# Attention scores of two heads in one product: keys in two zero-padded slots, heads rearranged between row halves

## The chip, the cores and the metric

The kernel runs on one core of a Trainium2 chip. The core has a matrix engine (TensorE, PE in the profile; PEld are its weight loads), VectorE (DVE), ScalarE (ACT), GpSimd (POOL) and a queue engine (SyncE, SP) that issues most transfers. A matrix product reads a stationary operand (`lhsT`) and a moving operand (`rhs`) from on-chip memory, contracts over the partitions, which are the rows of the array, and writes to PSUM; the columns of the stationary operand become the partitions of the output. The metric is the time of one execution on the device in microseconds (us); lower is better.

## What is computed

A sparse attention of 8 batches with 8 heads each (576 positions, 64 elements per head), and behind it a mixture of 8 experts over its 4,608 rows. Heads 0 to 3 use a local mask (a position sees itself and the 31 before it), heads 4 to 7 a strided mask (it sees earlier positions of the same residue modulo 32).

```python
scores = scale * np.matmul(q, k.transpose(0, 1, 3, 2))
mask_local = (rel >= 0) & (rel < stride)
mask_strided = (rel >= 0) & (pos[None, :] % stride == pos[:, None] % stride)
...
attn = np.exp(scores - max) / sum
x = (attn @ v) as rows of 512
out[do_compute] = xc + gate * (relu(xc @ w1[e]) @ w2[e])
```

## The kernel before

Positions of the strided heads are stored by residue, so that both masks become bands: a local block is 64 queries against a window of 96 keys (9 blocks), a strided block is 54 queries against 54 keys (11 blocks of three residues). The heads of one kind come in four to a batch and lie in a tile as two row halves `i` (partitions 0 to 63 and 64 to 127) times two columns `j`. A batch is cut into four units, `UNITS`: local blocks 0 to 4, local 5 to 8, strided 0 to 5, strided 6 to 10; unit (b, pr) is piece pr of batch b. All 32 units go through the same stages:

- `qk` makes the scores S: for each block four products, one per head, with 64 rows of contraction, 64 output columns and 96 or 54 moving columns (line 186). The four use the four quarters of the array, since head (i, j) reads row half i and writes output half i^j. The output has two PSUM banks (bank j) and one buffer. VectorE adds the mask (lines 193 and 195) and reduces the maximum (201), GpSimd subtracts it (204).
- `tex` transposes the differences on TensorE (224), ScalarE takes exp (232) into `ptl` or `pts`. For the strided kind two blocks stand in the 64-wide slots of `frame` and are transposed together; the odd block of the last unit has two transposes of its own.
- `pv` multiplies with the values and a column of ones (258). VectorE divides by the sum (266, 267, 273) into `x`.
- `xpose` transposes `x` (300), `score` computes gate logits from it (325), `route1` and `route2` make the slot of every row, and `scat` writes slot tables by indirect transfers of GpSimd (419).

The loop over units (from line 787) issues `qk` two units ahead (`LA = 2`): at unit n stand, on TensorE, S of unit n+2, then transposes of n, PV of n-1, transposes of the outputs of n-2. The order on TensorE, VectorE and GpSimd is as the code is written (`manual_schedule`); an engine waits at its next instruction until what it needs is there.

Loads stand in SP's queue in program order. A tile of queries and one of keys for each batch and kind come from one pool of six buffers (`part`, line 144), so three pairs are held; `loadq` (157) and `loadk` (162) issue two transfers each, one per `j` over 128 partitions. At odd units the loop loads the pair that is used three units later. `loadv` (167) loads values one batch ahead. Each transfer waits also for the transfer eight earlier (`DMAHW`), so at most eight are in flight. After the attention the feed-forward part runs (lines 603 to 605); the weights of the first expert are loaded during the last batches of the attention.

```python
p = slice(HP * i, HP * i + HP)
T.matmul(s[HP * (i ^ j):HP * (i ^ j) + HP, j, (blk - b0) * win:(blk - b0 + 1) * win],
         lhsT=qt[p, j, blk * nq:blk * nq + HP], rhs=kt[p, j, blk * nq:blk * nq + win],
         start=True, stop=True)
```

Of the kernel before, what the change touches and what calls it, by code (L numbers as in the profile page):

```python
# [23 lines left out]
HP = 64  # L24
# [73 lines left out]
def attn_moe(ctx: ExitStack, tc: tile.TileContext, q, k, v, w9d, w1d, w2d, cst, out, NB=B):  # L98
# [41 lines left out]
    frame = [ap.tile([128, 2, 6, HP], F32, name=f"frame{i}") for i in range(2)]  # L140

    qt_, kt_, vt_ = {}, {}, {}

    def part(d, L, kind, name):
        t = zp.tile([128, 2, S + PAD], F32, name=f"{name}{kind}", tag="qk", bufs=6)[:, :, 0:L[kind]]
        return t, d[:, :, kind * L[0]:kind * L[0] + L[kind]].rearrange("j p c -> p j c")

    def qtile(b, kind):
        qt_[b, kind], d = part(q[b], QL, kind, "qt")
        return qt_[b, kind], d  # L150

    def ktile(b, kind):
        kt_[b, kind], d = part(k[b], KL, kind, "kt")
        return kt_[b, kind], d

# [6 lines left out]
    def loadk(b, kind):  # L162
        t, d = ktile(b, kind)
        for j in range(2):
            nc.sync.dma_start(t[:, j], d[:, j])
# [10 lines left out]
    def qk(b, pr):  # L176
        kind, b0, b1 = UNITS[pr]
        qt, kt = qt_[b, kind], kt_[b, kind]
        nq, win = ((HP, LW), (SQ, SQ))[kind]
        n = (b1 - b0) * win  # L180
        s = ps("S", 2)
        for blk in range(b0, b1):
            for j in range(2):
                for i in range(2):
                    p = slice(HP * i, HP * i + HP)
                    T.matmul(s[HP * (i ^ j):HP * (i ^ j) + HP, j, (blk - b0) * win:(blk - b0 + 1) * win],  # L186
                             lhsT=qt[p, j, blk * nq:blk * nq + HP], rhs=kt[p, j, blk * nq:blk * nq + win],
                             start=True, stop=True)
# [13 lines left out]
        e = sw if kind == 0 else frame[pr - 2][:, :, 0:b1 - b0, 0:win]  # L202
# [6 lines left out]
    def tex(b, pr):  # L209
        kind, b0, b1 = UNITS[pr]  # L210
        e = e_.pop((b, pr))
        if kind == 0:
            pt = ap.tile([LW, 5 * 2 * 128], F32, name="ptl", tag="ptl", bufs=2)
            jobs = [(e[:, j, blk, :], LW) for blk in range(b1 - b0) for j in range(2)]
        else:
            pt = ap.tile([128, 3 * 2 * 128], F32, name="pts", tag="pts", bufs=2)
            fr = frame[pr - 2]
            jobs = [(fr[:, j, 2 * p:2 * p + 2, :].rearrange("p n w -> p (n w)")[:, 0:w], w)
                    for p in range((b1 - b0 + 1) // 2) for w in [HP + SQ if 2 * p + 1 < b1 - b0 else SQ] for j in range(2)]
        for g in range(0, len(jobs), 4):  # L220
            t = ps("T")
            part = jobs[g:g + 4]
            for x, (a, w) in enumerate(part):
                T.transpose(t[:w, x * 128:(x + 1) * 128], a, ident)  # L224
            yield
            x = 0
            while x < len(part):
                w = part[x][1]
                y = x
                while y < len(part) and part[y][1] == w:  # L230
                    y += 1
                A.activation(pt[:w, (g + x) * 128:(g + y) * 128], t[:w, x * 128:y * 128], AF.Exp, scale=0.125)
                x = y
        pt_[b, pr] = pt.rearrange("p (n j i q) -> p n j i q", j=2, i=2, q=HP)
# [3 lines left out]
    def pv(b, pr):  # L238
# [7 lines left out]
        if kind == 0:  # L246
            jobs = [(0, LW, m, j, j, m) for m in range(n) for j in range(2)]
            slots = (n, n)
            outs = [x[:, :, 64 * j:64 * j + 64] for j in range(2)]
        else:  # L250

            jobs = [(HP * o, HP * o + SQ, m, j, o, 2 * m + j) for m in range((n + 1) // 2)
                    for o in range(2) for j in range(2) if 2 * m + o < n]
            slots = (n + 1) // 2 * 2, n // 2 * 2
            outs = [x[:, o::2, :].rearrange("p m (j d) -> p m j d", j=2) for o in range(2)]
# [808 lines left out]
```

## Time and profile before

| | |
|---|---|
| median of 3 runs | 451.42 us (451.34 to 454.69) |
| the profiled execution | 449.82 us, of which the span of the profile is 448.2 us |
| mean granted TensorE clock | 0.975 |
| attention | up to about 181.5 us of the span |
| feed-forward | 181.5 to 448 us |

The profile lists every instruction with its start and duration; a group such as `x48` is 48 records, and a product of 32-bit floats leaves two records on TensorE (640 score products, 1,280 records). The chain of waits is followed back from the last instruction: each step names what released the next one; "issue" in it is time in which the engine waited for nothing that the profile shows. The DMA share is the mean busy share of 16 transfer engines.

### The profile page before, as it was taken

How to read it: one execution, taken by the hardware profiler on the slowest of the kernel's cores; microseconds unless marked ns; L12 is line 12 of the kernel's file. 1: busy time of each engine (PE TensorE's matmuls, PEld its weight loads, DVE VectorE, ACT ScalarE, POOL GpSimd, SP SyncE). 2: the span in 40 equal slices, each digit the busy share in tenths (PEclk: the TensorE clock that was granted, in tenths of full speed). 3: DMA queues.
4: the chain of work that ended last, by engine and by line, in shares of the span. 5: the costliest groups of instructions: out<-in, count | busy, mean ns of one | idle time of the engine just before them, and what ended most of it. 6: DMA issues, size and time to landing. Idle time of an engine off the chain costs nothing.

```text
span 448.2 us, 12126 instructions
## 1 busy us (share of the span) xinstructions
PE 413.8 (92%) x4951; PEld 370.7 (83%) x4952; DVE 257.6 (57%) x521; ACT 187.3 (42%) x366; POOL 163.9 (37%) x205
## 2 busy tenths in 40 slices
PE   6989889988878888899999999999999999999995
PEld 3867768766666666789899799999999999999984
DVE  3675667666857864481477465464474564756611
ACT  1345344533443625551543343444444444544400
POOL 3443236663658584464024318014024022200201
PEclk9799999998999879999999999999999999999999
DMA  8999999989798324532547466446566466645201
GB/s 298 398 393 335 361 322 351 289 261 317 211 348 261 102 57 108 147 67 79 181 158 220 149 217 207 153 159 207 171 197 184 159 200 198 214 157 158 73 21 42
DMA packets 53465, 91.09 MB, mean 203 GB/s; under 512 B 9272, under 2 KB 29624, under 8 KB 53406
## 3 DMA queue, kind: packets, MB, share of 16 engines
q1 hardware_dynamic: 45725, 79.86, 54.4%
q0 software_dynamic: 7680, 10.42, 8.3%
q8 instruction: 40, 0.66, 0.6%
q14 instruction: 20, 0.16, 0.1%
HBM read 75.22 MB, written 15.63 MB: 203 GB/s over the span
## 4 chain that ended last, share of the span: by engine, by line
PE 80%; DMA 7%; issue 5%; ACT 2%; DVE 2%; SPq 1%; POOL 1%; POOLq 0%; DVEq 0%; ACTq 0%
PE S L603 16%; PE S L605 16%; PE S L604 16%; PE PV L258 8%; PE S L186 5%; PE T L224 5%; DMA vt<-in_vp_dram 5%; PE T L300 4%; PE T L325 3%; PE PV L695 2%; PE T L597 2%; DMA kt<-in_kp_dram 2%; DMA xg<-out_dram,tab 1%; ACT s L330 1%; ACT xT L302 1%
## 5 line engine op out<-in xcount | busy, mean ns | idle before, releaser
L683 POOL DMA_INDIRECT out_dram<-ot,tab x25 | 28.0, 1120 | 150.7 <-DVE ot L681 142.1
L603 PE MATMUL S<-xh,w1h 128*128 128x342 f32 (+6 forms) x248 | 78.6, 317 | 0.2 <-DVE hl L616 0.2
L605 PE MATMUL S<-xh,w1l 128*128 128x342 f32 (+6 forms) x248 | 76.6, 309 | 0.0
L604 PE MATMUL S<-xl,w1h 128*128 128x342 f32 (+6 forms) x248 | 76.5, 308 | 0.0
L603 PE MATMUL S<-hh,w2h 128*128 128x288 f32 (+5 forms) x192 | 59.4, 309 | 0.0
L604 PE MATMUL S<-hl,w2h 128*128 128x288 f32 (+5 forms) x192 | 57.9, 302 | 0.0
L605 PE MATMUL S<-hh,w2l 128*128 128x288 f32 (+5 forms) x192 | 57.9, 302 | 0.0
L615 ACT ACTIVATE hh<-S 128x342 fp32r<-128x342 f32 (+6 forms) x64 | 28.0, 437 | 64.0 <-PE S L605 57.0
L541 DVE TENSOR_TENSOR w1l<-raw,w1h 128x1024 fp32r<-128x1024 f32 x32 | 40.4, 1266 | 22.0 <-ACT w1h L535 19.2
L603 PEld LDWEIGHTS S<-xh,w1h 128*128 128x128 f32 x248 | 46.8, 189 | 1.2 <-issue 0.6
L604 PEld LDWEIGHTS S<-xl,w1h 128*128 128x128 f32 x248 | 46.9, 189 | 0.1
L605 PEld LDWEIGHTS S<-xh,w1l 128*128 128x128 f32 x248 | 46.8, 189 | 0.0
L541 DVE TENSOR_TENSOR w2l<-raw,w2h 128x1024 fp32r<-128x1024 f32 x32 | 39.0, 1223 | 10.3 <-ACT w2h L535 10.1
L419 POOL DMA_INDIRECT table<-pay,rdi x38 | 40.3, 1060 | 12.1 <-issue 8.8
L575 POOL DMA_INDIRECT xg<-out_dram,tab x25 | 32.6, 1304 | 33.2 <-DMA out_dram<-ot,tab 9.9
L186 PE MATMUL S<-kt,qt 64*64 64x54 f32 (+1 forms) x1280 | 34.6, 245 | 9.2 <-issue 4.4
L616 DVE SCALAR_TENSOR_TENSOR hl<-S,hh 128x342 fp32r<-128x342 f32 (+6 forms) x64 | 31.0, 484 | 20.8 <-ACT hh L615 18.0
L186 PEld LDWEIGHTS S<-kt,qt 64*64 64x64 f32 x1280 | 28.1, 142 | 16.3 <-issue 6.8
L204 POOL TENSOR_TENSOR sm<-sm,mx 128x480 f32<-128x480 f32 (+1 forms) x32 | 28.4, 911 | 27.1 <-DVE mx L201 20.6
L603 PEld LDWEIGHTS S<-hh,w2h 128*128 128x128 f32 x192 | 36.2, 188 | 0.1
L604 PEld LDWEIGHTS S<-hl,w2h 128*128 128x128 f32 x192 | 36.3, 189 | 0.0
L605 PEld LDWEIGHTS S<-hh,w2l 128*128 128x128 f32 x192 | 36.2, 189 | 0.0
(159 smaller groups left out, 782.6 us busy)
## 6 DMA issues: line engine op xcount, KB each, us to landing
raw<-in_w_dram SPq DMA_DIRECT2D x64, 512.0 KB
vt<-in_vp_dram SPq DMA_DIRECT2D x40, 390.0 KB
qt<-in_qp_dram SPq DMA_DIRECT2D x16, 304.0 KB
kt<-in_kp_dram SPq DMA_DIRECT2D x16, 297.0 KB
out_dram<-x SPq DMA_DIRECT2D x16, 288.0 KB
kt<-in_kp_dram SPq DMA_DIRECT2D x14, 304.0 KB
qt<-in_qp_dram SPq DMA_DIRECT2D x14, 288.0 KB
out_dram<-x SPq DMA_DIRECT2D x32, 99.0 KB
```

Of the source, the lines that this page charges most:

```text
L186: T.matmul(s[HP * (i ^ j):HP * (i ^ j) + HP, j, (blk - b0) * win:(blk - b0 + 1) * win], lhsT=qt[p, j, blk * nq:blk * nq + HP], rhs=kt[p, j ...
L204: G.tensor_tensor(e[:, j], sw[:, j], mx[:, j].unsqueeze(2).broadcast_to([128, b1 - b0, win]), op=ALU.subtract)
L258: T.matmul(p[HP * i:HP * i + HP, bank, slot * 65:slot * 65 + 65], lhsT=pt[a:z, m, j, i ^ j, :], rhs=vt[a:z, (b0 if kind == 0 else b0 // 2) ...
L419: i = G.indirect_dma_start(out=table, out_offset=bass.IndirectOffsetOnAxis(ap=di[:, t:t + 1], axis=0), in_=pay[:, t, :], in_offset=None, b ...
L541: V.tensor_tensor(lo, raw_.pop((key, j)), hi.bitcast(F32), op=ALU.subtract)
L575: i = G.indirect_dma_start(out=xg[:s["P"], t, :], out_offset=None, in_=out[0:last, :], in_offset=bass.IndirectOffsetOnAxis(ap=s["tab"][:s[ ...
L603: T.matmul(p, lhsT=a[0], rhs=b[0], start=start, stop=False)
L604: T.matmul(p, lhsT=a[0], rhs=b[1], start=False, stop=False)
L605: T.matmul(p, lhsT=a[1], rhs=b[0], start=False, stop=stop)
L615: A.activation(s["hh"][:, f, :C], p[:, :C], AF.Relu)
L616: V.scalar_tensor_tensor(s["hl"][:, f, :C], p[:, :C], 0.0, s["hh"][:, f, :C].bitcast(F32), op0=ALU.max, op1=ALU.subtract)
L683: i = G.indirect_dma_start(out=out, in_=ot[:P], in_offset=None, bounds_check=NTOK - 1, oob_is_err=False, out_offset=bass.IndirectOffsetOnA ...
```

## The change

Keys get one tile per kind, `kz`, instead of a buffer of the pool: 128 partitions, two columns `j`, two slots `i`. Row half i holds its keys in slot i, and zeros stand in the other slot (four memsets, two by GpSimd, two by VectorE, once at the start). One product now contracts over all 128 rows with the queries of both halves and has the two slots as its moving operand, so that it gives the scores of two heads side by side: 192 or 108 moving columns instead of 96 or 54, two products for a block instead of four, each with 64 output columns (output half j). The heads in `q` and `k` are laid out so by the host (`pack`). Scores are stored in `segments`, (block, head) one after the other over the two banks; a block whose two segments fall into different banks (one local block of unit 0, one strided block of unit 3) keeps four products with half the rows.

`loadk` writes 64 partitions per transfer, both `j`. As each kind has one key tile, its next load waits until the products of the last unit that reads it are done, and is written behind that unit's `qk` in the program (`loadk(1, 0)` behind the two first `qk`, the loop's at the end of the odd unit). `loadq` keeps three buffers of its own. `tex` of the strided kind transposes slots 2m and 2m+1, two heads of one block: five transposes in the last unit of a batch instead of six. `pv` takes the matching order, and in the last unit of a batch VectorE has one pair of small operations for the sums (lines 266 and 267) where it had two.

```diff
-    frame = [ap.tile([128, 2, 6, HP], F32, name=f"frame{i}") for i in range(2)]
+    frame = [ap.tile([128, 12, HP], F32, name=f"frame{i}") for i in range(2)]
...
+    kz = [zp.tile([128, 2, 2, n], F32, name=f"kz{kind}") for kind, n in enumerate(KL)]
...
+        qt_[b, kind] = t = zp.tile([128, 2, S + PAD], F32, name=f"qt{kind}", tag="qt", bufs=3)[:, :, 0:QL[kind]]
...
-    def loadk(b, kind):
-        t, d = ktile(b, kind)
-        for j in range(2):
-            nc.sync.dma_start(t[:, j], d[:, j])
+    def loadk(b, kind, c=slice(0, None)):
+        d = k[b][:, :, kind * KL[0]:kind * KL[0] + KL[kind]].rearrange("j p c -> p j c")
+        for i in range(2):
+            p = slice(HP * i, HP * i + HP)
+            nc.sync.dma_start(kz[kind][p, :, i, c], d[p, :, c])
+
+    def segments(pr):
+        _, b0, b1 = UNITS[pr]
+        seq = [(blk, i) for blk in range(b0, b1) for i in range(2)]
+        if pr == 0:
+            seq.insert(b1 - b0, seq.pop(1))
+        return {x: divmod(f, b1 - b0) for f, x in enumerate(seq)}
...
         for blk in range(b0, b1):
+            (x, at), (x1, _) = seg[blk, 0], seg[blk, 1]
             for j in range(2):
+                if x == x1:
+                    T.matmul(s[HP * j:HP * j + HP, x, at * win:(at + 2) * win], lhsT=qt[:, j, blk * nq:blk * nq + HP],
+                             rhs=kt[:, j, :, blk * nq:blk * nq + win], start=True, stop=True)
+                    continue
                 for i in range(2):
...
+                    p, c = slice(HP * i, HP * i + HP), i ^ j
+                    x, at = seg[blk, i]
+                    T.matmul(s[HP * c:HP * c + HP, x, at * win:(at + 1) * win], lhsT=qt[p, c, blk * nq:blk * nq + HP],
+                             rhs=kt[p, c, i, blk * nq:blk * nq + win], start=True, stop=True)
+                x, x1 = 0, 1
...
-            jobs = [(fr[:, j, 2 * p:2 * p + 2, :].rearrange("p n w -> p (n w)")[:, 0:w], w)
...
+            jobs = [fr[:, 2 * HP * m:2 * HP * m + HP + SQ] for m in range(b1 - b0)]
...
+    for kind in range(2):
+        G.memset(kz[kind][0:HP, :, 1], 0.0)
+        V.memset(kz[kind][HP:128, :, 0], 0.0)
...
-    loadk(1, 0)
     loadv(0, 1)
...
     run(qk(0, 1))
+    loadk(1, 0)
...
                 loadq(g // 2, g % 2)
-                loadk(g // 2, g % 2)
...
         run(*rank, *late, *front)
+        if pr % 2 and n // 2 + 3 < 2 * NB:
+            loadk((n // 2 + 3) // 2, (n // 2 + 3) % 2)
```

How the program order changes on two engines. First TensorE around the strided units of batch 1 and the first unit of batch 2, before (S are scores, T transposes or small sums, PV the products with values; a row is a run of equal instructions, and `64x54` is output partitions times moving columns):

```order
L186 MATMUL S<-kt_250,qt_247 64x54 x24
L224 MATMUL T<-cs,sm_80 96x128 x10
L258 MATMUL PV<-vt_134,pts 64x65 x20
L300 MATMUL T<-cs,x_437 128x128 x6
L186 MATMUL S<-kt_250,qt_247 64x54 x20
L224 MATMUL T<-cs,sm_81 96x128 x8
L258 MATMUL PV<-vt_196,ptl 64x65 x20
L300 MATMUL T<-cs,x_437 128x128 x5
L186 MATMUL S<-kt_406,qt_403 64x96 x20
```

The same place after the change:

```order
L188 MATMUL S<-kz_87,qt_224 64x108 x12
L235 MATMUL T<-cs,sm_80 96x128 x10
L256 MATMUL PV<-vt_137,pts 64x65 x20
L292 MATMUL T<-cs,x_385 128x128 x6
L188 MATMUL S<-kz_87,qt_224 64x108 x4
L194 MATMUL S<-kz_87,qt_224 64x54 x4
L188 MATMUL S<-kz_87,qt_224 64x108 x4
L235 MATMUL T<-cs,sm_81 96x128 x8
L256 MATMUL PV<-vt_185,ptl 64x65 x20
L292 MATMUL T<-cs,x_385 128x128 x5
L194 MATMUL S<-kz_86,qt_363 64x96 x4
L188 MATMUL S<-kz_86,qt_363 64x192 x8
```

The stages stand in the same order. Inside a score stage there are half as many products of twice the moving columns, and in units 0 and 3 of a batch a run of four products of the old form stands ahead of the others or between them.

Second SP's queue in the first microseconds, before (`kt_131` are the keys of batch 1, local, `vt_134` the values of batch 0, strided, `vt_196` those of batch 1, local, `kt_250` the keys of batch 1, strided):

```order
L165 DMA kt_131<-in_kp_dram 128x608 [waits DMAHW0_49]
L165 DMA kt_131<-in_kp_dram 128x608 [waits DMAHW1_49]
L172 DMA vt_134<-in_vp_dram 128x780 [waits DMAHW2_49]
L172 DMA vt_134<-in_vp_dram 128x780 [waits DMAHW3_49]
L172 DMA vt_196<-in_vp_dram 128x780 [waits DMAHW4_49]
L172 DMA vt_196<-in_vp_dram 128x780 [waits DMAHW5_49]
L172 DMA vt_196<-in_vp_dram 128x780 [waits DMAHW6_49]
L160 DMA qt_247<-in_qp_dram 128x608 [waits DMAHW7_49,PE_49]
L160 DMA qt_247<-in_qp_dram 128x608 [waits DMAHW0_49]
L165 DMA kt_250<-in_kp_dram 128x594 [waits DMAHW1_49]
L165 DMA kt_250<-in_kp_dram 128x594 [waits DMAHW2_49]
```

And after the change (`kz_86` is the local key tile, `kz_87` the strided one, `vt_137` the values of batch 0, strided, `vt_185` those of batch 1, local):

```order
L173 DMA vt_137<-in_vp_dram 128x780 [waits DMAHW2_49]
L173 DMA vt_137<-in_vp_dram 128x780 [waits DMAHW3_49]
L159 DMA kz_86<-in_kp_dram 64x2x608 [waits DMAHW4_49,PE_49]
L159 DMA kz_86<-in_kp_dram 64x2x608 [waits DMAHW5_49]
L173 DMA vt_185<-in_vp_dram 128x780 [waits DMAHW6_49]
L173 DMA vt_185<-in_vp_dram 128x780 [waits DMAHW7_49]
L173 DMA vt_185<-in_vp_dram 128x780 [waits DMAHW0_49]
L153 DMA qt_224<-in_qp_dram 128x608 [waits DMAHW1_49]
L153 DMA qt_224<-in_qp_dram 128x608 [waits DMAHW2_49]
L159 DMA kz_87<-in_kp_dram 64x2x594 [waits DMAHW3_49,PE_49]
L159 DMA kz_87<-in_kp_dram 64x2x594 [waits DMAHW4_49]
```

The keys of batch 1, local, have moved behind two transfers of values, and the loads of keys wait for TensorE where the loads of queries did.

96 lines of the change are left out of this document (36 added, 60 removed).

## The prediction, made before the changed kernel ran

> **What bounds the kernel now.** I read the page first (span, busy shares, slices, chain), then a table of stretches, one for each batch of the attention, then TensorE's waits between 27 and 160 us, then the chain in order of time.
>
> ```profile
> span 448.2 us, 12126 instructions
> PE 413.8 (92%) x4951; PEld 370.7 (83%) x4952; DVE 257.6 (57%) x521; ACT 187.3 (42%) x366; POOL 163.9 (37%) x205
> PE   6989889988878888899999999999999999999995
> DMA  8999999989798324532547466446566466645201
> PE 80%; DMA 7%; issue 5%; ACT 2%; DVE 2%; SPq 1%; POOL 1%; POOLq 0%; DVEq 0%; ACTq 0%
> ```
>
> TensorE is busy 92% of the span and makes 80% of the chain that ended last. In the slices (11.2 us each) it is at eight or nine tenths from the second on, but in the first nine slices the transfer engines are as full. So two things could set the pace of the attention.
>
> ```profile
> core 0: us, PE busy (x) PEld busy (x) DVE busy (x) ACT busy (x) POOL busy (x), PEclk, DMA share, GB/s
> 0.00:27.40 27.40, 21.48 (x405) 16.05 (x407) 15.88 (x30) 7.03 (x14) 12.29 (x31) 0.88 0.96 355
> 27.40:45.40 18.00, 17.15 (x386) 13.71 (x386) 10.51 (x25) 8.46 (x19) 6.21 (x8) 1.00 1.01 356
> 45.40:64.90 19.50, 17.65 (x399) 13.90 (x399) 11.79 (x26) 9.00 (x21) 6.21 (x8) 1.00 1.00 344
> 128.70:153.90 25.20, 20.21 (x411) 16.07 (x409) 19.61 (x52) 11.44 (x26) 16.76 (x26) 0.93 0.70 222
> ```
>
> Each stretch runs from one batch's first strided scores to the next's. From 27.4 us a batch takes 18.0 to 19.5 us, TensorE is busy 17.15 and 17.65 us of it, VectorE 10.5 to 11.8. The transfer share is 1.0 in both, so I looked at who waits for a transfer.
>
> ```profile
> PE PV L258 <- issue: 5.7, 10, 1.4
> PE S L186 <- issue: 3.8, 6, 1.8
> PE T L224 <- issue: 2.3, 6, 1.1
> PE T L300 <- issue: 0.7, 2, 0.6
> PE S L186 <- DMA kt<-in_kp_dram: 0.5, 1, 0.5
> ```
>
> Between 27 and 160 us TensorE lost 0.5 us to a load and 5.7 + 3.8 + 2.3 + 0.7 = 12.5 us to "issue", which the profile ties to nothing. So TensorE's own instructions set the pace there, with the transfers close behind. Before 27.4 us it is the other way round:
>
> ```profile
> 12.35 7.24 DMA vt<-in_vp_dram
> 19.60 7.65 DMA kt<-in_kp_dram
> 27.39 0.91 PE S L186 x44
> ```
>
> The chain goes through loads until the strided keys of batch 1 land; the scores at 27.39 us waited for them.
>
> **The change, part by part.** The scores first. Prices come from the chain in order of time, where a stage of each size stands (start, us, records):
>
> ```profile
> 45.43 0.85 PE S L186 x48
> 49.46 0.73 PE S L186 x40
> 54.74 0.99 PE S L186 x40
> 61.83 0.82 PE S L186 x32
> 39.38 1.94 PE T L325 x16
> 114.13 1.32 PE PV L258 x40
> 56.42 1.08 PE PV L258 x32
> ```
>
> The local stages (96 columns) of 40 and 32 records differ by 0.17 us for 8 records: four records, one in each quarter of the array, take 0.085 us. The strided ones (54 columns, 48 and 40 records) give 0.12 / 2 = 0.060 us for four. A block has eight records, so 0.17 and 0.12 us. What is left of a stage, 0.99 - 10 x 0.085 = 0.14 us, is its start and the turn to the next stage.
>
> The new form (128 rows, 64 output columns) is not in the trace with 192 or 108 columns, but two products of that form are. The gate logits (L325, 288 columns) take 1.94 / 8 = 0.243 us for two records side by side in the two column halves, and the local PV (L258, 96 rows, 65 columns) 0.24 / 4 = 0.060 us. Between them a column costs 0.183 / 223 = 0.00082 us, so 192 columns come to 0.164 us and 108 to 0.095 us a pair. The ends: 0.060 us a pair, if width cost nothing, and 0.243; they would make a batch 0.4 us shorter or 6.2 us longer and belong to the rivals that are faster or don't overlap. I take the line between them, since one form gives both points and both new widths lie between. A new block has two pairs: 0.328 instead of 0.17 us (local), 0.190 instead of 0.12 (strided). So half the instructions take longer: two heads contract over 64 rows each, and half of the moving columns are now zeros.
>
> A batch has 8 local and 10 strided blocks of the new form: 8 x 0.158 + 10 x 0.070 = 1.96 us. The two blocks that keep four products change the array's division three times more in a batch. No row isolates that; the 0.14 us left over holds one turn and more, so it lies between 0 and 0.14, and I take 0.09: 0.27 us. The strided transposes of the last unit fall from six to five:
>
> ```profile
> 66.89 1.25 PE T L224 x10
> 70.82 1.01 PE T L224 x8
> ```
>
> One transpose is (1.25 - 1.01) / 2 = 0.12 us. Together 1.96 + 0.27 - 0.12 = 2.11 us of TensorE more in a batch; the products with values are as many as before and each still fills the quarters it filled.
>
> The other edits. VectorE loses two operations a batch:
>
> ```profile
> 69.99 0.12 DVE L266 TENSOR_SCALAR rc<-PV 128x4 f32<-128x4 f32 x1
> 70.14 0.18 DVE L267 RECIPROCAL rc<-rc 128x4 f32<-128x4 f32 x1
> ```
>
> That is 0.3 us on an engine busy 10.5 of 18.0 us: I take 0, with 0.3 a batch as the most. The memsets stand before any score:
>
> ```profile
> 0.88 1.41 POOL L784 MEMSET frame<- 128x768 f32 x2 [0.29 <-POOLq L1050]
> 0.97 0.11 DVE L756 MEMSET dummy<- 128x64 uint32 x1 [0.85 <-PEq L1050]
> 5.01 1.33 PEld L186 LDWEIGHTS S<-kt,qt 64*64 64x64 f32 x40 [1.18 <-issue]
> ```
>
> GpSimd clears 768 elements in 0.7 us, so 1,216 in 1.1. VectorE's row gives at most 0.11 / 64 x 1,216 = 2.1 us for the local tile, ending at 3.2 us. The first scores wait for keys until 5.01 us, so this costs 0; without that cover at most 2.1.
>
> The key loads. The local keys of batch 1 now stand behind two value loads, 390 KB each: 2.2 us at the 355 GB/s of the first stretch. These rows show sizes and the place:
>
> ```profile
> vt<-in_vp_dram SPq DMA_DIRECT2D x40, 390.0 KB
> ...
> kt<-in_kp_dram SPq DMA_DIRECT2D x14, 304.0 KB
> ...
> 18.35 1.34 PE L186 MATMUL S<-kt,qt 64*64 64x96 f32 x40
> 22.20 0.89 PE L186 MATMUL S<-kt,qt 64*64 64x96 f32 x32
> 26.56 0.32 PE L186 MATMUL S<-kt,qt 64*64 64x54 f32 x4 [0.64 <-issue]
> ```
>
> The first scores of batch 1 start at 18.35 + 2.2 us; that stage and the next are 0.7 and 0.6 us longer; the strided scores, which could begin at 26.56 but had their keys at 27.39, begin at 26.56 + 2.2 + 0.7 + 0.6 = 30.1. That is 2.7 us late (0 at least, if the loads have room; 3.5 at most, if those scores had nothing to spare). The transfer share of 0.96 there says that they have little room, so I take 2.7. From there a key load is asked for when its tile is free, a little later than now:
>
> ```profile
> 24.91 1.10 SPq L165 DMA_DIRECT2D kt<-in_kp_dram  x2
> 36.32 0.89 PE L186 MATMUL S<-kt,qt 64*64 64x96 f32 x27 [0.37 <-issue]
> ```
>
> The keys of batch 2 were issued 11.4 us before use; the longest step of a load in the chain is 7.65 us. The new program issues the load when the scores three units ahead are done, about 13 us at 4.5 us a unit, so I cost it at 0. If the cover were gone TensorE would wait at the scores, and behind the waiting load stand SP's value loads and stores.
>
> The sum: 2.7 at the start; the strided half of batch 1, 10 x 0.07 + 0.18 - 0.12 = 0.8; six batches x 2.11 = 12.7. Together 16.2 us on TensorE. What gives way? The "issue" waits, 12.5 us, could shrink, as TensorE asks for fewer instructions and loads less often per microsecond; 0 to 12.5 us. The stretch from 128.7 us is the nearest row: with the transfer share at 0.70 TensorE still idles 5.0 of 25.2 us, so emptier transfers alone do not remove idle time. I take 4, nearer the low end. So 449.8 (the profiled execution; 1.6 us of it outside the span) + 16.2 - 4 = 462.0; the median of the runs is 1.6 us above that execution: 463.6 us. The bounds of the start (0 to 3.5), of the turns (0 to 0.42 a batch) and of what gives way (0 to 12.5) reach from 455 to 469.
>
> **The rivals.**
>
> Absorbed: all 12.5 us of "issue" goes. For it: TensorE waits there for nothing visible, beside full transfers. Against it: the idle time in the stretch with 0.70. It gives 449.8 + 16.2 - 12.5 + 1.6 = 455.1.
>
> Transfers become the bound: if a load to 64 partitions runs at half rate. A key pair (two loads of 297 or 304 KB) takes 1.7 us more at 355 GB/s. Four of them before the strided scores of batch 1 make 6.8, of which half falls beside TensorE's own delay there, so +3.4; later two pairs a batch make 3.4 against TensorE's 2.1, +1.3 for each of the four batches in which the transfers are full. That gives 463.6 + 3.4 + 5.2 = 472. For it: shares of 1.00 and 1.01. Against: no row times such a load, and eight are in flight at once. The Trainium skill, page "SBUF — State Buffer", section on the DMA port swizzle, says that partitions 0 to 63 reach 8 of 16 ports; no run here shows it yet.
>
> Faster: records cost by their number, not their width. 468 fewer score records from 27.4 us on (26 of 32 units, 576 in all) at 0.021 us (the mean of 0.99 / 40 and 0.85 / 48) save 9.8 us: 451.4 - 9.8 = 441.6. It decides at a pair of 192 columns taking 0.085 us. Against: 288 columns take 0.243 and 65 take 0.060. The Trainium skill, page "TensorE: Matmul & The Clock Gate", section "Wait — 56ns, not 53.3ns?", has a floor of about 25 ns from one matmul's start to the next, by which 576 records would be worth 14.4 us; here 48 records took 0.85 us, 18 ns each, so this trace is below that floor and the measurement decides.
>
> No overlap: the two column halves don't run side by side for the new form, as they write one bank. A block then costs 0.656 or 0.380: 8 x 0.328 + 10 x 0.190 = 4.5 us a batch more, 6.4 batches, 28.9: 492. Against: L325 also writes both halves of one tile, at half the time that its columns would need one after the other.
>
> **How the numbers follow.** Likeliest case 0.56, transfers 0.20, absorbed 0.14, faster 0.06, no overlap 0.04. The time is the likeliest case's, 463.6; its own range is 458 to 469. The range 455 to 474 reaches from the absorbed case to the transfer case and leaves out the two outer ones and tails. A measurement here can tell about 1%, 4.5 us: slower than 455.9 holds the likeliest, transfers and no-overlap cases, 0.80; within 1% most of the absorbed case and a tail, 0.14; faster 0.06.
>
> **What would show it.** In the new profile: score stages of the local units at 1.3 to 1.6 us and of the strided ones at about 1.0 to 1.2, half as many records; batches from 27 us on at about 20 to 21.5 us; strided scores of batch 1 near 30 us. The prediction is wrong if a 192-column pair takes much less than 0.164 us, if TensorE waits for keys by whole microseconds (transfers), or if "issue" almost vanishes (absorbed).

## The result, and the profile after

| | before | after |
|---|---|---|
| median of 4 runs each | 451.38 us (450.69 to 454.69) | 470.47 us (466.44 to 472.68) |
| the profiled execution | 449.82 us, span 448.2 us | 472.68 us, span 471.0 us |
| mean granted TensorE clock | 0.975 | 0.964 |

The changed kernel takes 1.0377 times as long, with a 95% interval of 1.0294 to 1.046: it is slower, by 19.1 us in the medians. The prediction was 463.6 us with a range of 455 to 474. The profiled execution is the slowest of the four runs of the changed kernel, so its trace shows 22.8 us more span, not 19. All ratios here leave disturbed runs out, which is why a ratio and the quotient of two medians can differ.

First the page of the changed kernel: the span, the busy shares, the slices (now 11.8 us each) of TensorE and of the transfer engines, and the chain that ended last.

```profile
span 471.0 us, 10947 instructions
PE 432.3 (92%) x4367; PEld 380.1 (81%) x4368; DVE 259.4 (55%) x507; ACT 186.7 (40%) x366; POOL 166.2 (35%) x207
PE   6779999987969797799899999999999999999994
DMA  8999999989999984233255646746656566645201
PE 66%; DMA 17%; DVE 5%; issue 4%; ACT 3%; SPq 2%; POOL 1%; another core or an unknown queue 1%; POOLq 0%; DVEq 0%; ACTq 0%
```

TensorE is busy 92% of the span, as before, and 584 matmul records are gone, yet it is busy 432.3 us instead of 413.8. The chain tells more than the share: transfers carry 17% of it where they carried 7%, TensorE 66% where it was 80%. The transfer slices stand at eight or nine tenths up to the fifteenth, 177 us, where before they thinned out after the thirteenth, 146 us.

The stretches of the changed kernel, with the columns of the table in the prediction. Each again runs from one batch's first strided scores to the next's, so the borders are later than before:

```profile
0.00:27.40 27.40, 17.17 (x160) 11.05 (x163) 11.94 (x20) 3.84 (x7) 10.84 (x22) 0.94 0.95 267
...
36.80:55.40 18.60, 18.33 (x314) 14.27 (x314) 12.25 (x25) 9.17 (x21) 6.42 (x9) 1.00 1.03 291
55.40:75.60 20.20, 19.65 (x322) 15.14 (x322) 11.61 (x24) 8.70 (x21) 6.20 (x8) 1.00 0.99 281
145.10:169.60 24.50, 21.73 (x336) 16.48 (x334) 18.23 (x48) 11.53 (x26) 15.98 (x24) 0.93 0.98 266
169.60:201.30 31.70, 24.37 (x351) 19.29 (x349) 18.04 (x56) 13.49 (x33) 20.15 (x28) 0.79 0.49 132
```

The last two columns are the lesson. The share is as full as before (0.95 to 1.03), but what is moved fell: 267 GB/s instead of 355 in the first 27.4 us, 291 and 281 instead of 356 and 344 in the next two batches. Transfer engines can be busy all the time and move a fifth to a quarter less.

From these borders the 22.8 us of the trace split up. The strided scores of batch 1 start at 36.8 instead of 27.4 us: +9.4. From there to the strided scores of batch 7 it is 169.6 - 36.8 = 132.8 us instead of 153.9 - 27.4 = 126.5: +6.3 for six batches. The last stretch up to the feed-forward part takes 31.7 us; before it took

```profile
153.90:181.60 27.70, 23.18 (x393) 18.09 (x391) 17.24 (x59) 12.87 (x31) 17.90 (x23) 0.88 0.35 89
```

27.7 us: +4.0. The feed-forward part takes 471.0 - 201.3 = 269.7 instead of 266.6 us: +3.1.

The chain of the changed kernel in order of time (start, us, what) shows the start, and the size of the new score stages:

```profile
5.88 7.16 DMA qt<-in_qp_dram
...
13.05 6.92 DMA qt<-in_qp_dram
...
19.98 10.50 DMA vt<-in_vp_dram
...
30.50 10.30 DMA qt<-in_qp_dram
...
46.94 8.35 DMA kz<-in_kp_dram
...
55.42 1.33 PE S L188 x24
...
91.53 1.45 PE S L188 x16
...
96.50 1.26 PE S L188 x24
```

Up to 41 us nearly every step is a load that waits for an earlier load, and single loads take 7 to 10.5 us where the longest step in the chain before was 7.65. The stage of 16 wide local records (four blocks) takes 1.45 us, which is the prediction's 4 x 0.328 + 0.14; six strided blocks take 1.26 to 1.33 us, where 6 x 0.190 + 0.14 = 1.28 was priced.

Last TensorE's waits between 27 and 175 us in the changed kernel (us in total, times, longest):

```profile
PE S L194 <- DMA kz<-in_kp_dram: 1.9, 2, 1.1
...
PE PV L256 <- issue: 1.4, 4, 0.4
PE T L337 <- issue: 1.2, 1, 1.2
PE T L235 <- issue: 0.7, 3, 0.3
PE S L188 <- DMA kz<-in_kp_dram: 0.3, 1, 0.3
```

"Issue" is down from 12.5 to 1.4 + 1.2 + 0.7 = 3.3 us. At the start it is the keys that TensorE waits for. Between 5 and 40 us, in the changed kernel:

```profile
PE S L194 <- DMA kz<-in_kp_dram: 5.2, 4, 2.3
PE S L188 <- DMA kz<-in_kp_dram: 2.6, 1, 2.6
```

and in the kernel before:

```profile
PE S L186 <- DMA kt<-in_kp_dram: 2.5, 4, 1.5
```

That is 7.8 us instead of 2.5, one of the signs by which the prediction said it would be wrong (waits for keys by whole microseconds). So the wide products do cost what was priced, the batches grew by less than that, and the start grew by more than three times what was expected. Three theories could divide this up:

- **Loads**: a key load that fills only partitions 0 to 63, or 64 to 127, moves slower, and since the transfers were full this delays all the others.
- **Width**: the wide products carry most of the time, and the loads are late because the queue is.
- **One tile**: the single key tile per kind, whose load must wait for its last reader, carries it.

### The profile page after: what moved, and what is told of

Read it like the earlier page. It is cut to its first block, busy times and chain, and to the rows that moved or that the text cites. A ratio compares the mean times of both kernels' runs of the same rounds, so it can differ in the third digit from the quotient of the medians.

```text
span 471.0 us, 10947 instructions
## 1 busy us (share of the span) xinstructions
PE 432.3 (92%) x4367; PEld 380.1 (81%) x4368; DVE 259.4 (55%) x507; ACT 186.7 (40%) x366; POOL 166.2 (35%) x207
## 4 chain that ended last, share of the span: by engine, by line
PE 66%; DMA 17%; DVE 5%; issue 4%; ACT 3%; SPq 2%; POOL 1%; another core or an unknown queue 1%; POOLq 0%; DVEq 0%; ACTq 0%
PE S L595 14%; PE S L597 14%; PE S L596 14%; DMA qt<-in_qp_dram 5%; PE S L188 4%; PE PV L256 4%; DMA kz<-in_kp_dram 4%; DMA out_dram<-x 3%; PE T L235 3%; PE T L292 2%; DMA vt<-in_vp_dram 2%; PE T L317 2%; PE PV L687 2%; PE T L589 2%; DMA table<-pay,rdi 1%
## 5 line engine op out<-in xcount | busy, mean ns | idle before, releaser
L188 PE MATMUL S<-kz,qt 128*64 128x108 f32 (+1 forms) x576 | 49.4, 314 | 5.7 <-DMA kz<-in_kp_dram 2.9
L567 POOL DMA_INDIRECT xg<-out_dram,tab x25 | 34.2, 1369 | 37.0 <-DMA out_dram<-ot,tab 19.0
L188 PEld LDWEIGHTS S<-kz,qt 128*64 128x64 f32 x576 | 34.6, 145 | 14.8 <-POOL sm L214 2.9
L411 POOL DMA_INDIRECT table<-pay,rdi x38 | 39.2, 1031 | 12.5 <-issue 8.5
L592 DVE TENSOR_TENSOR xl<-T,xh 128x288 fp32r<-128x288 f32 (+7 forms) x30 | 13.5, 469 | 42.3 <-ACT xh L591 26.5
```

What stands on the lines that cost most here:

```text
L188: T.matmul(s[HP * j:HP * j + HP, x, at * win:(at + 2) * win], lhsT=qt[:, j, blk * nq:blk * nq + HP], rhs=kt[:, j, :, blk * nq:blk * nq + w ...
L411: i = G.indirect_dma_start(out=table, out_offset=bass.IndirectOffsetOnAxis(ap=di[:, t:t + 1], axis=0), in_=pay[:, t, :], in_offset=None, b ...
L567: i = G.indirect_dma_start(out=xg[:s["P"], t, :], out_offset=None, in_=out[0:last, :], in_offset=bass.IndirectOffsetOnAxis(ap=s["tab"][:s[ ...
```

## The experiments

The level of the kernel before differs between the sets of runs (451.38, 451.47, 444.92 and 443.24 us), so times are compared inside a set, and with the kernel before by ratio. A `+` or `-` in a diff is against the kernel named.

### Which partitions a load fills: e1 and e2

Both are the kernel before with its narrow products and its six buffers; only the loads of keys are cut another way. Each still issues two transfers of the same bytes. e1 gives each transfer 64 partitions, as the change does (the first keys, loaded ahead of the loop, are cut by halves too in e1, e6 and e7, and by every other partition in e2 and e9; the diffs leave that out):

```diff
     def loadk(b, kind):
-        for j in range(2):
-            nc.sync.dma_start(t[:, j], d[:, j])
+        for i in range(2):
+            p = slice(HP * i, HP * i + HP)
+            nc.sync.dma_start(t[p], d[p])
...
```

> The kernel before, with its key loads cut by row halves (64 partitions and both columns j a transfer, partitions 0 to 63 and then 64 to 127) instead of by column; products and buffers are untouched. Loads theory (a transfer into one half of the partitions moves at a lower rate): the rate between 6 and 27 us falls from 395 to about 290 GB/s, the strided scores of batch 1 start at 34 us or later instead of 27.4, and the kernel takes 457 to 466 us. Width theory (the wider products are the loss) and key-tile theory (the single key tile is): no change, 450 to 453 us.

e2 also gives each transfer 64 partitions, but every other one:

```diff
-            p = slice(HP * i, HP * i + HP)
+            p = slice(i, 128, 2)
...
```

> As the run with half loads, but each of the two transfers takes every other partition (0, 2, ... and 1, 3, ...): as many partitions, bytes and pieces in each, spread over the whole memory. Loads theory, if it is the half of the memory that counts: about 395 GB/s and 450 to 453 us again. If it is the number of partitions or the shape of the transfer that counts: slow like the run with half loads. Width and key-tile theories: 450 to 453 us.

e1 took 466.73 us (464.01 to 469.09; ratio 1.0491, 1.0327 to 1.0656), e2 451.51 us (449.59 to 453.78; ratio 1.0134, 1.0016 to 1.0251). The two ran on one chip, their runs don't overlap, and the difference is 15.2 us. e2's median is that of the kernel before there (451.47 us), by its ratio it lies 0.2 to 2.5% above it; e9 below is the closer test of that. e1 and e2 move the same bytes in the same number of transfers, in the same order, to the same number of partitions; only which partitions differs. The transfers between 6 and 27 us show it. First the kernel before:

```profile
DMA packets 3718, 8.29 MB, mean 395 GB/s; under 512 B 398, under 2 KB 880, under 8 KB 3716
```

The changed kernel:

```profile
DMA packets 3044, 6.22 MB, mean 296 GB/s; under 512 B 324, under 2 KB 1073, under 8 KB 3043
```

e1, with the rate in 40 slices of half a microsecond ahead of it:

```profile
GB/s 328 312 242 272 272 320 379 356 208 186 238 240 223 246 374 386 410 416 402 367 399 413 368 310 203 203 240 220 204 230 310 328 363 380 398 380 392 409 404 404
DMA packets 3205, 6.69 MB, mean 318 GB/s; under 512 B 344, under 2 KB 1067, under 8 KB 3203
```

And e2:

```profile
GB/s 313 375 388 328 292 323 351 381 362 307 360 390 407 410 404 402 401 395 423 427 376 392 391 412 414 402 392 392 392 404 410 385 395 411 374 383 381 398 401 378
DMA packets 3793, 8.04 MB, mean 383 GB/s; under 512 B 408, under 2 KB 1127, under 8 KB 3791
```

e1 falls twice to 186 to 246 GB/s, about half of the 400 around it, and e2 does not. Both stretches (10.2 to 13.4 and 18.6 to 21.8 us) lie inside steps of e1's chain in which a key load is under way:

```profile
6.99 6.78 DMA kt<-in_kp_dram
...
13.79 8.98 DMA kt<-in_kp_dram
```

e1's rate was expected at about 290 GB/s and its strided scores of batch 1 at 34 us or later; they start at 33.91 us, and its time is just above the 466 us that were the most expected. TensorE then waits for these keys; its waits in e1 between 27 and 165 us:

```profile
PE S L187 <- DMA kt<-in_kp_dram: 9.6, 10, 1.6
```

That line stood at 0.5 us in the kernel before, between 27 and 160 us. The rate agrees roughly with loads at half speed: a batch loads 2 x (304 + 288) KB of queries, 2 x (304 + 297) = 1,202 KB of keys and 5 x 390 KB of values, 4,336 KB in all. If the keys take twice their time, an estimate for the mean rate is 395 x 4,336 / (4,336 + 1,202) = 309 GB/s; e1 shows 318 and the changed kernel 296.

The Trainium skill, page "SBUF — State Buffer", section "Door 1: The DMA port swizzle", says that partitions 0 to 63 lie behind 8 of 16 ports, and partitions 64 to 127 behind the other 8. e1's slices at half the rate agree. The Trainium skill, the same page, section "Can I just issue two DMAs to hit both halves?", says that the only way to all 16 ports is one transfer over all 128 partitions. e2 shows that such a transfer is not the only one to keep the rate: 383 GB/s with transfers to 64 partitions, every other one, beside 395 in the kernel before.

### More loads cut so, and cut finer: e6 and e7

If the loads theory holds, cutting the query loads by halves as well must lower the rate further. e6 is e1 with

```diff
...
     def loadq(b, kind):
-        for j in range(2):
-            nc.sync.dma_start(t[:, j], d[:, j])
+        for i in range(2):
+            p = slice(HP * i, HP * i + HP)
+            nc.sync.dma_start(t[p], d[p])
...
```

> The run with half loads, with the loads of queries (nearly as many bytes) cut by row halves as well: the suspected cost twice. Loads theory: another 8 to 18 us on top of that run's 467, 475 to 485 us, and a rate below 290 GB/s between 6 and 27 us. If the half loads cost through something of the keys alone (their order or their place): 465 to 469 us.

It took 467.21 us (465.72 to 470.21; ratio 1.0636, 1.0431 to 1.084), and moved 289 GB/s between 6 and 27 us, less than e1's 318. So the rate fell as expected, but the time did not follow by the 8 to 18 us that were expected: by the ratios e6 lies some 6 us above e1, and the two intervals overlap.

e7 asks whether the halves could run side by side if they alternate in smaller pieces; it is e1 with

```diff
-        for i in range(2):
-            p = slice(HP * i, HP * i + HP)
-            nc.sync.dma_start(t[p], d[p])
+        for j in range(2):
+            for i in range(2):
+                p = slice(HP * i, HP * i + HP)
+                nc.sync.dma_start(t[p, j], d[p, j])
...
```

> The run with half loads, each key load cut in four (row half and column), the halves alternating in the queue in pieces of half the size. If transfers to the two halves overlap when they follow each other closely: 452 to 460 us. If each transfer keeps its lower rate whatever stands beside it: 465 to 472 us, as now or a little more for the eight in flight being smaller.

It took 460.04 us (458.27 to 463.12; ratio 1.0459, 1.0247 to 1.067) at 322 GB/s. The 460 us are at the edge of the range for loads that overlap, but that range was set for a kernel before at 451 us, and here it took 444.92. The ratio lies within e1's interval, and the rate is e1's: finer pieces don't help in any way that can be told. In the same set e6 lies 7.2 us above e7, but the two differ in the queries' halves and in the size of the pieces, so what the queries' halves cost in time is not shown.

### The rest of the change without loads and width: e5 and e8

e5 is the kernel before with one key tile per kind, loaded where the change loads it, over all 128 partitions:

```diff
-        t = zp.tile([128, 2, S + PAD], F32, name=f"{name}{kind}", tag="qk", bufs=6)[:, :, 0:L[kind]]
+        tag, n = ("qt", 3) if name == "qt" else (f"kt{kind}", 1)
+        t = zp.tile([128, 2, S + PAD], F32, name=f"{name}{kind}", tag=tag, bufs=n)[:, :, 0:L[kind]]
...
-    loadk(1, 0)
...
     run(qk(0, 1))
+    loadk(1, 0)
...
-                loadk(g // 2, g % 2)
...
+        if pr % 2 and n // 2 + 3 < 2 * NB:
+            loadk((n // 2 + 3) // 2, (n // 2 + 3) % 2)
```

> The kernel before with one key tile for each kind, loaded at the places of the changed program, but by column over all 128 partitions; products stay as before. If the single tile and the moved loads cost nothing: 450 to 454 us, so that the 10 us of the run with mixed rows are the wide products. If they are what is left there: 457 to 462 us, with waits for keys on TensorE.

446.61 us (439.48 to 446.85) against 444.92 us (437.22 to 448.29) before: the runs of both cover the same ground. It gave no interval; e9 below settles it.

e8 is the rest of the changed kernel: its layout of heads, five transposes and one pair of sums' operations, but narrow products whose scores lie by row half as before (so the places that `segments` gives go with the wide products), key buffers in the pool of six, loads at the old places and over all 128 partitions, no zeros:

```diff
...
-    kz = [zp.tile([128, 2, 2, n], F32, name=f"kz{kind}") for kind, n in enumerate(KL)]
+            kt_[b, kind] = zp.tile([128, 2, S + PAD], F32, name=f"kt{kind}", tag="qk", bufs=6)[:, :, 0:KL[kind]]
...
-            nc.sync.dma_start(kz[kind][p, :, i, c], d[p, :, c])
+                nc.sync.dma_start(t[:, j], d[:, j])
...
-                if x == x1:
+                if False:
...
```

> The rest of the change alone: heads rearranged, scores of two heads of a block side by side in the strided frames, five transposes instead of six, fewer small VectorE operations; four narrow products, six buffers, key loads by column and in the old places, no zeros. By the terms of the prediction 0.12 us of TensorE a batch goes and nothing is added: 449.5 to 452 us. If the rearrangement itself costs something: 454 us or more.

444.26 us (443.01 to 449.44; ratio 1.0134, 0.9907 to 1.0361): no difference that can be told, with an interval that still leaves room for up to 3.6%.

### Width and loads, each with and without the other: e3, e4, and e9 to e12

e3 is the changed kernel with four narrow products for every block; half-row loads, one tile and zeros stay:

```diff
-        return {x: divmod(f, b1 - b0) for f, x in enumerate(seq)}
+        return {(blk, i): (i, blk - b0) for blk, i in seq}
...
-                if x == x1:
+                if False:
...
-            e = frame[pr - 2][:, 0:2 * (b1 - b0), 0:win].rearrange("p (j n) w -> p j n w", j=2)
+            e = frame[pr - 2][:, 0:2 * (b1 - b0), 0:win].rearrange("p (n j) w -> p j n w", j=2)
```

> The changed kernel, with its loads and single key tiles, but four products with 64 rows for every block as before the change (bank by row half). Loads theory: still slow, 459 to 468 us, strided scores of batch 1 at 33 us or later. Width theory: back near the kernel before, 451 to 454 us. Key-tile theory: slow as well, but with the start of batch 1 within 2 us of the kernel before.

e4 is the changed kernel with its wide products, but a pair of heads shares the partitions alternately, so that a key load fills every other one. Zeros must then be set over whole slots ahead of the first loads, which wait for them, and the blocks that are split contract over 128 rows too:

```diff
-            p = slice(HP * i, HP * i + HP)
+            p = slice(i, 128, 2)
             nc.sync.dma_start(kz[kind][p, :, i, c], d[p, :, c])
... (the products of the blocks that are split)
-        G.memset(kz[kind][0:HP, :, 1], 0.0)
-        V.memset(kz[kind][HP:128, :, 0], 0.0)
+        G.memset(kz[kind][:, :, 1], 0.0)
+        V.memset(kz[kind][:, :, 0], 0.0)
... (the layout of the rows)
```

> The changed kernel, with the rows of the two heads of a tile alternating, so that each key load takes every other partition; products stay as wide (the blocks that straddle banks get products with one slot each), key tiles stay single. The zeros then cover whole slots, and the first key loads wait for them (about 1 to 2 us at the start). Loads theory: most of the loss goes, 454 to 461 us, strided scores of batch 1 at 29 to 31 us. Width theory: as slow as the changed kernel, 466 to 472 us. Key-tile theory: 464 to 470 us, with waits for keys in the later batches.

On one chip with e1 and e2, e3 took 468.15 us (466.64 to 471.22; ratio 1.0534, 1.0381 to 1.0688) and e4 461.53 us (459.1 to 462.37; ratio 1.0379, 1.0284 to 1.0475). So without its wide products the changed kernel gains nothing (its own ratio was 1.0377), and with wide products and loads at 360 GB/s it lies 6.6 us below e3. That spoke for loads, but only in part: e4 lies just above the 461 us that the loads theory allowed, its strided scores of batch 1 start at 33.0 us where 29 to 31 were expected (e3's at 36.5), and the changed kernel itself had run on another chip, with a ratio equal to e4's. The last set therefore ran all four combinations on one chip, all with one key tile per kind. e9 is e5 with key loads to every other partition:

```diff
-        for j in range(2):
-            nc.sync.dma_start(t[:, j], d[:, j])
+        for i in range(2):
+            p = slice(i, 128, 2)
+            nc.sync.dma_start(t[p], d[p])
...
```

> The kernel before with one key tile per kind and key loads by every other partition: narrow products, loads at full width. Theory (the half-row loads carry the cost): within 6 us of the kernel before, and 10 to 18 us below the same arrangement with half-row loads (e11). Rival (the single key tile carries part of it): more than 8 us above the kernel before.

e10 is the changed kernel, with no edit:

> The changed kernel itself, beside the next two and e9 on one chip, so that two products or four, and half-row loads or alternate ones, can be set against each other: half rows and wide products here. Theory (costs overlap): within 3 us of e11, which has four narrow products, and 5 to 10 us above e12, which has alternate rows. Rival (costs add up): 6 to 9 us above e11 and 13 to 17 us above e12.

e11 is e3 again:

> The changed kernel with four narrow products for every block, half-row loads kept. Theory (costs overlap): within 3 us of e10, 10 to 18 us above e9. Rival (costs add up): 6 to 9 us below e10.

e12 is e4 again:

> The changed kernel with its wide products and key loads by every other partition. Theory (costs overlap): 5 to 10 us below e10, and 6 to 10 us above e9, of which some 4 us are the start, where the first loads wait for the zeros. Rival (width is hidden where loads are on time): within 5 us of e9.

| | loads to every other partition | loads to 64 partitions in a row |
|---|---|---|
| four narrow products | e9: 442.03 us (439.96 to 451.2), ratio 1.0008 (0.996 to 1.0055) | e11: 462.5 us (460.96 to 464.84), ratio 1.0504 (1.0422 to 1.0587) |
| two wide products | e12: 450.93 us (448.37 to 453.58), ratio 1.0236 (1.0147 to 1.0325) | e10: 463.83 us (459.49 to 468.0), ratio 1.0492 (1.0391 to 1.0593) |

The kernel before took 443.24 us there. Read along the rows, half-row loads cost 20.5 us with narrow products and 12.9 with wide ones. Read down the columns, wide products with all that e4 brings cost 8.9 us where loads are at full width, and 1.3 us where they are not: nothing that can be told. Adding the two single costs would give 442.03 + 20.5 + 8.9 = 471.4 us; measured is 463.83. The costs overlap by 7.6 us.

By the ratios the four differences are 0.050, 0.026, 0.023 and -0.001 of the kernel before (22, 11, 10 and -0.5 us), and the overlap is 0.024, some 11 us. Two things make these differences less clean than the table looks. e11 differs from e9 also in the layout and the zeros, for which e8 and the last timeline below show no cost; the clean pair for the loads is e1 and e2, with 15.2 us. And only e12 holds its first loads up for zeros, so up to 2.7 us of the overlap (its delay at the start, below) can be that.

The expectation that they overlap held; e10 lay 12.9 us above e12 where 5 to 10 were expected, at the edge of the additive theory's 13 to 17, and e11 20.5 above e9 where 10 to 18 were: the loads cost more than the theory had.

Where the time goes is seen in the six batches from the first strided scores of batch 1 to those of batch 7, the same work in each run, by the columns as above. e9:

```profile
29.50:147.40 117.90, 104.74 (x2383) 83.56 (x2382) 85.91 (x214) 57.84 (x132) 65.57 (x91) 0.98 0.95 304
```

e12:

```profile
32.20:155.00 122.80, 113.92 (x1946) 90.13 (x1945) 86.14 (x202) 57.77 (x132) 66.75 (x92) 0.99 0.92 293
```

e11:

```profile
35.20:165.30 130.10, 109.78 (x2377) 86.97 (x2375) 85.38 (x203) 56.83 (x131) 67.04 (x92) 0.94 0.98 271
```

e10 (its profiled execution, 468.0 us, is the slowest of its six):

```profile
36.80:168.50 131.70, 117.64 (x1944) 90.58 (x1943) 86.47 (x202) 56.94 (x131) 65.47 (x92) 0.98 0.99 265
```

With full-width loads, wide products make TensorE busy for 9.2 us more, and 4.3 us of idle time go (13.2 to 8.9): 4.9 us. With half-row loads it is 7.9 us more busy and 6.3 less idle (20.3 to 14.1): 1.6 us. So there is more idle time for wide products to fill where the loads are slow. The half-row loads (e11 against e9) add 7.2 us of idle time and 5.0 us of busy time for the same products; the granted clock of that stretch is 0.94 instead of 0.98. So part of what they cost comes through a lower clock; whether the idle time brings it about is not shown.

The first strided scores of batch 1 and of batch 7 on TensorE's timeline give the pace (start, us; the edge of the queried window cuts some rows short, so only the starts are read). e9:

```profile
29.47 0.74 PE L188 MATMUL S<-kt,qt 64*64 64x54 f32 x36
...
147.40 0.90 PE L188 MATMUL S<-kt,qt 64*64 64x54 f32 x24 [0.99 <-DVE sm L195]
```

e12:

```profile
32.21 1.33 PE L188 MATMUL S<-kz,qt 128*64 128x108 f32 x24
...
154.97 1.35 PE L188 MATMUL S<-kz,qt 128*64 128x108 f32 x12 [0.94 <-DVE sm L199]
```

e11:

```profile
35.24 0.32 PE L194 MATMUL S<-kz,qt 64*64 64x54 f32 x2
...
165.32 1.64 PE L194 MATMUL S<-kz,qt 64*64 64x54 f32 x48 [0.94 <-DMA out_dram<-x]
```

Six batches take 117.9 us in e9, 122.8 in e12 (+4.9) and 130.1 in e11 (+12.2). Batch 1 starts 2.7 us later in e12 and 5.8 us later in e11. So half-row loads cost 2 us a batch and near 6 at the start; wide products, with loads at full width, 0.8 us a batch. In e10 the two starts are 36.78 and 168.52, so six batches take 131.7 us (+13.8 against e9).

The waits of TensorE between 27 and 165 us for "issue" in e9:

```profile
PE PV L260 <- issue: 2.3, 2, 1.8
PE T L226 <- issue: 1.8, 5, 0.8
...
PE T L302 <- issue: 0.4, 1, 0.4
```

and in e12:

```profile
PE T L233 <- issue: 0.7, 3, 0.2
```

Of 4.5 us, 0.7 are left. In e11 they are 12.1 us, and only 1.5 us there are put down to keys, where e1 had 9.6: there the cost of slow loads shows little as waits for a load.

No kernel here is faster than the kernel before by more than its interval. Wide products with two key tiles per kind were not tried. Nor were e4's zeros set without holding the first loads up, so how much of e12's 2.7 us at the start is theirs stays open.

## Why the prediction was right, and where it was not

The sign was right and the time lay in the range, 6.9 us above the number. But the mechanism held to be likeliest, TensorE paying for wide products, is not what sets the time: with the half-row loads, e11 with narrow products is as slow as e10 with wide ones. The transfers rival, with a chance of 0.20 and 472 us, comes nearest. e12 is close to what the likeliest case priced, wide products with loads that keep their rate: it took 0.0236 more than the kernel before, or 10.7 us on 451.4, where 12.2 were forecast. The changed kernel's time came so near to the forecast by luck: loads that were costed at nothing cost more than the whole forecast, and then hid most of the cost that was forecast.

- **The step that failed: the key loads.** The prediction said of a key load "so I cost it at 0", looking only at when it is issued, and left its rate to a rival. With narrow products, half-row loads cost 15.2 us (e1 against e2) to 20.5 (e11 against e9), more than the whole predicted increase of 12.2. The rival sized them at 3.4 us at the start and 1.3 a batch, for four batches, on top of TensorE's own; they cost 5.8 at the start and 2.0 a batch by themselves. That its sum of 472 us lies near 470.47 is luck as well, since the two costs don't add. The argument against the rival, that no row times such a load and that eight are in flight at once, was no evidence: the transfers were already full before 27 us (a share of 0.96), so a lost rate had no room to hide in.
- **The start: 2.7 taken, 9.4 measured** in the changed kernel. The term held only the new order of the loads. e5 and e9, with that order and loads that keep their rate, start the strided scores of batch 1 at 28.0 and 29.5 us, 0.6 and 2.1 after the 27.4 of the kernel before (on other chips), so the order costs no more than was taken. The rate is the rest: in the chain the loads up to 41 us follow each other at 7 to 10.5 us, and with half-row loads the same scores start at 35.2 (e11) and 36.8 us (e10).
- **The price of a wide product: right.** 0.164 and 0.095 us a pair give the stages of 1.45 and 1.28 us, and the trace has 1.45 and 1.26 to 1.33. The straight line between two measured products of the same form was a good price. The rivals that priced records by number, or without overlap of the column halves, fall with it.
- **Six batches: 12.7 less 4 taken, 6.3 measured.** The stretch from the first strided scores of batch 1 to those of batch 7, first before, then after:

```profile
27.40:153.90 126.50, 110.08 (x2381) 87.90 (x2381) 84.22 (x214) 56.47 (x130) 65.41 (x91) 0.97 0.90 295
...
36.80:169.60 132.80, 120.43 (x1946) 92.44 (x1945) 84.76 (x203) 56.48 (x131) 64.90 (x90) 0.97 0.98 268
```

TensorE idles 12.4 us of it instead of 16.4: 4.0 us, the size taken for what gives way, though "issue" alone fell by more than that and waits for keys, VectorE and ScalarE came in its place. The score products alone are busy for 39.4 us instead of 24.7, so 14.7 more where 6 x 2.23 = 13.4 were priced. But TensorE as a whole is busy for only 10.4 us more, since the products with values, which the prediction left as they were, take 27.8 us instead of 31.2, and the transposes, gate logits and small sums 60.2 instead of 61.2 (each counted by itself; they overlap a little). e12 against e9 shows the same: scores +13.3, values -2.0, all of TensorE +9.2, idle time -4.3, in all +4.9. So the price and the idle time were right, and the term missed is the time that the products with values lose; why they are shorter is not shown. The absorbed rival was right that "issue" goes (12.5 to 3.3), but not about the total.
- **The sum of the costs.** Even a right size for the loads would have misled if added: loads and width share the same time, and one hides 5 to 11 us of the other (7.6 by the medians, 11 by the ratios, less up to 2.7 for e12's zeros). The prediction had the loads on top of the width; the experiments show width nearly free on top of the loads.
- **Slips in the prediction's own figures.** Its three bounds (start, turns, what gives way) reach down to about 450.6 us when all are taken at their low ends (451.4 + 16.2 - 2.7 - 1.8 - 12.5); the 455 is the absorbed case alone. And 1.0 to 1.2 us for the strided stages doesn't fit its price, by which six blocks take 1.28; measured are 1.26 to 1.33.
- **What was costed at 0 and cost nothing that could be told.** One key tile, loaded in the new places: e9 at 1.0008 (0.996 to 1.0055), with loads to every other partition. Layout, transposes and VectorE's operations: e8 at 1.0134 (0.9907 to 1.0361), within its wider interval. The zeros in the changed kernel end before the first scores; the timeline there (start, us):

```profile
0.88 2.13 POOL L762 MEMSET kz<- 64x1216 f32 x2 [0.29 <-POOLq L1047]
...
2.66 1.05 DVE L763 MEMSET kz<- 64x1188 f32 x1 [0.20 <-issue]
...
5.08 0.55 PE L194 MATMUL S<-kz,qt 64*64 64x96 f32 x2 [0.35 <-DMA kz<-in_kp_dram]
```

The last ends at 3.71 us, the first scores start at 5.08.

- **Not foreseen and not explained:** +4.0 us in the last stretch and +3.1 in the feed-forward part of the profiled execution. In the last stretch of the attention the granted clock was 0.79 instead of 0.88, and TensorE was busy 24.37 us instead of 23.18. From e9 to e10 the same two parts grow by only about 0.4 and 1.9 us. No experiment took this apart.

## What to carry to other kernels

When a layout is changed, ask which partitions each transfer fills before asking when it is issued: key loads as two transfers to 64 partitions in a row each cost 15 to 20 us here, where the same bytes to every other partition cost nothing that could be told (e9). A full transfer share says that the engines are busy, not that they move much, so read the GB/s beside it. And where two things are near to being the bound, price each by itself and together: here the one that set the pace hid much of the other, and the sum of the single costs was too high.

## What the hardware showed that was not expected

- With key loads to 64 partitions in a row, the rate of everything in flight falls to 186 to 246 GB/s in two stretches between 6 and 27 us, inside the steps of key loads, though loads over all partitions stand beside them in the same queue; with every other partition it is 383 GB/s on average (e1 and e2).
- With half-row loads and narrow products the mean granted clock is lower in the runs: 0.951 to 0.967 in e11 and 0.959 to 0.969 in e1, against 0.967 to 0.987 in e9 and 0.973 to 0.983 in e2. With half-row loads and wide products (e10) it is 0.969 to 0.981.
- The "issue" waits are not a fixed property of a program. Between 27 and about 160 us they were 12.5 us in the kernel before, 4.5 in e9, which has the same products and whose times equal those of the kernel before on its chip, 12.1 in e11, 3.3 in the changed kernel and 0.7 in e12. What they wait for isn't shown by any trace here.
- The same kernel before ran at 451 us in two sets of runs and at 443 to 445 in two others. A difference of 1.5% between kernels can be read only from runs of one set.
